# Gated mix of two attentions: exponents' tiles in one pool from the start, and additions of branch A moved to GpSimd

## The chip, the core and the metric

The kernel runs on one core of a Trainium2 chip. A core has TensorE (PE in the profile; its weight loads are the row PEld), VectorE (DVE), ScalarE (ACT), GpSimd (POOL) and SyncE (SP), which mostly issues DMAs; each works through a queue of its own in the order in which the program was written, and waits on semaphores for the others. SBUF is the working memory, PSUM (eight banks of 128 x 512 f32) takes what TensorE writes. The metric is the device time of one execution in microseconds, lower is better.

## The reference

x is 2048 x 512, and all is f32. Branch A is an attention in which each position looks at eight earlier ones, two apart; branch B has 32 heads of queries on one head of keys and values, over all 2048 positions. A gate from x mixes the two:

```python
def _A_ref(x, wqkv, wo):              # H = 32, Dh = 16, W = 8, dil = 2
    ...
    idx = pos[:, None] - off[None, :]
    ...
    logits = jnp.einsum("bhsd,bhswd->bhsw", q, kg) * scale
    logits = jnp.where(mask[None, None, :, :], logits, -1e9)
    attn = _softmax(logits, axis=-1)
    o = jnp.einsum("bhsw,bhswd->bhsd", attn, vg)
    ...
def _B_ref(x, wq, wk, wv, wo):        # one k and one v for all 32 heads
    ...
    scores = jnp.einsum("bhqd,bkd->bhqk", q, k) * (Dh ** -0.5)
    p = _softmax(scores, axis=-1)
    o = jnp.einsum("bhqk,bkd->bhqd", p, v)
    ...
g = _sigmoid((x * gate_w).sum(-1, keepdims=True))
return g * a + (1 - g) * b
```

## The kernel before

**Stages.** (1) Loads of x and weights; x and the weights are split into a high part and the rest (`xh`, `xl`, `wqh`, `wql`, `wah`, `wal`), so that three products in the fast f32r form replace one in f32. (2) The "front": `lumps` is a list of 14 projections of branch B's queries and 64 of branch A (`gg`, a group of eight heads, times `j`, one of 16 groups of positions). Each is 12 products whose two halves of 64 rows run beside each other into the two halves of one of the PSUM tiles `eb[0]`, `eb[1]` (`pe` in the profile). (3) 512 steps: in step s two pairs of score products go to `eb[0]` and `eb[1]` (`exp_pair`, L425), ScalarE takes their exponents into a tile `pexp` (L427), and the weighted sum of the step before (`weighted`, L435) adds four heads' products with `vst` in `po`. Sixteen steps make a unit: four heads of 512 queries, 32 units in all. (4) Four out phases (`out_phase`) between steps project finished rows and store them; a short tail does the last four row groups.

**Maxima.** The softmax of branch B needs each row's maximum first. These 2048 products (L301) are filled in wherever TensorE and the banks `m2` (`pm`) and `m1` (`ps`) are free, beside the front, the steps and the out phases; DVE reduces each straight from PSUM (L322 for a pair, L333 for a single one). In the front, once `half_keys` has formed half sums and half differences of keys (`kcd`), two blocks of keys are done in one: ScalarE takes the absolute value of a difference (L384, `dd`), and DVE adds the sum and reduces (L394). When a unit's maxima are complete, `filled` reduces and transposes them, and `shift_a`, `shift_c` and `shift_b` split them into two parts and write them with eight small DMAs (L414) into rows of the unit's query tile, where the score products subtract them. `stack(u)` loads a unit's query tile `qst` from DRAM (`qd`) with four DMAs on SP's queue; `queries_out` writes `qd` on the same queue.

**Branch A.** A projection's two halves are added by `a_post`: ScalarE copies one half from PSUM (L238), DVE adds the other (L243) into a `stage` tile of two positions, which an ACT-queue DMA stores to DRAM (`ad`). GpSimd then works through branch A's scores and values (`work`, a generator cut into pieces with costs in ns), for 32 pieces (g, hf); per piece DVE does the maximum over the eight positions (`a_max`) and the sum and reciprocal (`a_sum`, L530, L531), ScalarE the exponent.

**Order.** Nothing is scheduled at run time. A planner in the kernel's own Python keeps clocks for TensorE, ScalarE, DVE and GpSimd (`clk`, `pool`), times when banks come free (`free`) and tasks with due times (`tasks`, `hooks`), and writes each engine's instructions in the order that follows. `stream` interleaves the front or an out phase with maxima. `settle(kind, n)` runs tasks of a kind at once until n are left.

**Memory.** `xh` has four tiles of its own in pool `p1`, which is released when the front ends; the six `pexp` tiles of 128 x 1024 belong to a pool that is opened after that. The first step's exponents therefore go to a tile `early` that takes the place of `xh0`:

```python
if x == last and i == 4:
    early.append(p1.tile([P, 2, 2, 512], F32, name="early", tag="xh0", bufs=1))
    exp_pair(0, 0, early[0][:, 0])
```

Of the kernel before, what the change touches and what calls it, by code (L numbers as in the profile page):

```python
# [22 lines left out]
HG = 4  # L23
# [25 lines left out]
def gated_mix_kernel(ctx, tc, xt, wa, wk, wq, wo_a, wo_b, out):  # L49
# [64 lines left out]
    def split_x(t, eng):  # L114
        for c in range(C):
            split(xh[t][:, c, :], xl[:, t, c, :], xraw[t, c], eng)
# [64 lines left out]
    def queries(m):  # L181
        qb, cc = divmod(m, NHG // 2)
        cs = slice(cc * P, (cc + 1) * P)
        return three(lambda c: wqh[:, c, cs], lambda c: wql[:, c, cs], lambda c: xh[qb][:, c, :], lambda c: xl[:, qb, c, :])
# [9 lines left out]
    def queries_post(m, bank):  # L194
# [11 lines left out]
        def rest():  # L206
            nonlocal pool
            nc.scalar.activation(hi, own, AF.Copy)
            nc.gpsimd.tensor_sub(lo, own, hi.bitcast(F32))
# [10 lines left out]
    def a_project(gg, j):  # L220
        n = GN + (0 if gg else VN)
        t, r = j // 4, slice(j % 4 * P, (j % 4 + 1) * P)
        return three(lambda c: xh[t][:, c, r], lambda c: xl[:, t, c, r], lambda c: wah[gg][:, c, :n], lambda c: wal[gg][:, c, :n])

    def a_post(gg, j, x):

        bank, n = eb[x], GN + (0 if gg else VN)
        settle("post0", 0)
        settle("post1", 0)
# [4 lines left out]
        if gg == 0 and j < 3:  # L234
# [5 lines left out]
        free[f"e{x}"] = at + 1.5  # L240

        def rest():
# [4 lines left out]
            free[f"e{x}"] = after("dve", at, 0.5 if gg else 0.75) + 0.1  # L247
            if j % 2 == 1:
                dst = ad[gg * GC:(gg + 1) * GC, HALO:, :].rearrange("g (p j) n -> p g (j n)", j=NJ)
                tasks.append((free[f"e{x}"], lambda: nc.scalar.dma_start(dst[:, :, (j - 1) * AN:(j + 1) * AN], st.rearrange("p g j n -> p g (j n)")), (), "store"))  # L250
            if j == NJ - 1:
                tasks.append((free[f"e{x}"] + 0.5, whole, (gg,)))

        tasks.append((at, rest, (), f"post{x}"))

    def gates():
# [4 lines left out]
        for i in range(HG):  # L261
            for b in range(4):
                nc.scalar.activation(gate_t[32 * i:32 * i + 32, :, :, b], gate[32 * b:32 * b + 32, 1, :].rearrange("p (q j) -> p q j", j=4), AF.Copy)
# [74 lines left out]
    sel, kcd, dd, pend, ready_d, formed = [], [], [], [], [0.0, 0.0], set()  # L338
# [15 lines left out]
    def half_keys(g):  # L354
# [6 lines left out]
        clk["pe"] += 1.2  # L361
        for x in range(2):
            parts, src = kcd[0][:, g, x], hb[g][x]
            nc.scalar.activation(parts, src, AF.Identity, scale=mk[:, 0:1])
            at = after("act", clk["pe"] + T_LAT, 0.6)
            nc.vector.scalar_tensor_tensor(parts, src, mk[:, 1:2], parts.bitcast(F32), op0=ALU.mult, op1=ALU.add)
# [38 lines left out]
    def shift_c(v, mt, th, ml):  # L405
        nc.vector.scalar_tensor_tensor(ml, mt, mk[:, 5:6], th.bitcast(F32), op0=ALU.mult, op1=ALU.add)
        after("dve", 0, 0.45)
# [10 lines left out]
    pe, pexp, exped, early = [], {}, {}, []  # L418

    def exp_pair(s, pr, e=None):  # L420
# [5 lines left out]
        e = e or pe[0].tile([P, 2, 512], F32, name="pexp", bufs=6)  # L426
# [101 lines left out]
    def a_sum(g):  # L528
        asum[g] = p2[0].tile([P, NH, AG], F32, name="asum", bufs=2)
        nc.vector.tensor_reduce(asum[g], alog[g].rearrange("p w j h -> p j h w"), AX.X, ALU.add)  # L530
        nc.vector.reciprocal(asum[g], asum[g])  # L531
        after("dve", 0, 0.6)
# [107 lines left out]
    def stream(seq, mm, done, pooled):  # L640

        at, told = [0, 0], 0
        while min(at) < len(seq):
# [20 lines left out]
            if paired():  # L664
# [9 lines left out]
    def out_phase(js, n):  # L674

        prepare(js[0], n)
        turn(js[0], 1)
        later.pop(js[0])()
# [119 lines left out]
    def work():  # L798

        def sub(g, hf):  # L800
# [3 lines left out]
            hooks.append((pool + 5000, a_sum, g, ("sum", g, hf)))  # L804
            yield 500

        def values(g, hf):
            yield lambda: ("sum", g, hf) in done and (g < 8 or p2b)
# [11 lines left out]
        extra = list(wos)  # L820
        yield from load(0)
        yield from load(1)
        for i in range(0, len(order), 2):
            yield from a_scores(*order[i])
            hooks.append((pool + 3500, a_max, order[i][0], ("max",) + order[i]))
            for k, x in enumerate(a_scores(*order[i + 1])):
                yield x
                if k == 8:
                    yield from sub(*order[i])
            hooks.append((pool + 3500, a_max, order[i + 1][0], ("max",) + order[i + 1]))  # L830
            for k, x in enumerate(values(*order[i])):
                yield x
                if k == 8:
                    yield from sub(*order[i + 1])
            yield from load(i + 2)
# [36 lines left out]
    def mm(b, at):  # L872
# [3 lines left out]
        if x not in items:  # L876
# [10 lines left out]
            elif x == last:  # L887
                formed.clear()
            items[x] = queries(lump[1]) if lump[0] == "q" else a_project(*lump[1:])
            clk["pe"] = max(clk["pe"], free[f"e{x % 2}"])  # L890
# [3 lines left out]
        nc.tensor.matmul(eb[x % 2][:, b, :n], l[h], r[h], start=(i == 0), stop=(i == 3 * C - 1))  # L894
        return T_R if n == 512 else 0.18

    def done_mm(at):
# [7 lines left out]
        if x == last and i == 4:  # L905
            early.append(p1.tile([P, 2, 2, 512], F32, name="early", tag="xh0", bufs=1))
            exp_pair(0, 0, early[0][:, 0])
# [7 lines left out]
        else:  # L915
            gg, j = lump[1:]
            a_post(gg, j, x % 2)
# [8 lines left out]

    stream([(x, i) for x in range(len(lumps)) for i in range(3 * C)], mm, done_mm, True)
    assert not pend
    clk["pe"] += 0.7
    settle("post0", 0)  # L930
# [112 lines left out]
```

## Time and profile before

| what | value |
|---|---|
| median of three runs | 1550.73 us (1546.35 to 1551.43) |
| the profiled execution | 1548.13 us, of which its span 1546.4 us |
| TensorE weight loads | 720.5 us busy |
| front | 30 to 289 us |
| first and last weighted sum of the steps | 293.2 and 1534.1 us |
| out phases begin near | 878, 1146, 1289 and 1446 us |
| branch A on GpSimd | 147 to about 1050 us |

The span runs from the first to the last instruction. A row of the windows gives start and end, length, and then for each engine its busy time in that stretch and, in brackets, how many instructions it began; then the mean clock that TensorE was granted (1 is full speed), the share of DMA time and GB/s. A row of the waits gives the engine and line that waited, what ended the wait, the total in us, how often, and the longest one. A row of the timeline gives start, duration, engine, line, operation and tiles; the brackets tell the idle time before it and what ended that. A matmul's end is modelled, so that products that overlap look longer than the distance between their starts.

### The profile page before, as it was taken

The numbers are of one execution on the slowest core, as the hardware profiler recorded it, in microseconds if no ns is written. First come the engines' busy times: TensorE is split into PE (matmuls) and PEld (weight loads), VectorE is DVE, ScalarE is ACT, GpSimd is POOL, SyncE is SP. The second block draws the span as 40 slices with busy tenths as digits, with TensorE's granted clock in tenths as the row PEclk, the third lists the DMA queues.
The fourth block names the chain that finished last, engine by engine and source line by source line (L and its number), as shares of the span: only waits on it lengthen the run. The fifth ranks groups of instructions, "written<-read, shape, count | busy, mean of one in ns | idle before, by whom it ended". The sixth has DMA issues, their size and how long they took to land.

```text
span 1546.4 us, 29008 instructions
## 1 busy us (share of the span) xinstructions
PE 1498.4 (97%) x11020; PEld 720.5 (47%) x11020; DVE 1290.7 (83%) x1937; ACT 1220.0 (79%) x1490; POOL 934.7 (60%) x1525
## 2 busy tenths in 40 slices
PE   7899999899999999999999999999999999999997
PEld 4788999533333333333333453333345335433532
DVE  6887888789888989989898898998889889887811
ACT  4447776589999989999899749989875985799686
POOL 7731898698898888888889888884022003100310
PEclk9999999899999999999999999999999999999999
DMA  6643243221121122112112112110000000000000
GB/s 213 186 115 120 88 149 92 70 75 47 40 74 57 39 75 74 47 40 74 40 39 72 57 41 72 40 40 11 12 18 23 11 2 15 15 1 1 1 1 28
DMA packets 44019, 85.63 MB, mean 55 GB/s; under 512 B 9616, under 2 KB 26072, under 8 KB 39784
## 3 DMA queue, kind: packets, MB, share of 16 engines
q0 software_dynamic: 6816, 37.97, 7.4%
q1 hardware_dynamic: 19160, 31.40, 6.8%
q10 hardware_dynamic: 17904, 14.42, 2.9%
q8 instruction: 86, 1.41, 0.4%
q14 instruction: 53, 0.43, 0.1%
HBM read 57.97 MB, written 25.25 MB: 54 GB/s over the span
## 4 chain that ended last, share of the span: by engine, by line
PE 87%; ACT 5%; DVE 5%; DMA 1%; POOL 1%; issue 1%; SPq 1%; DVEq 0%; ACTq 0%; POOLq 0%
PE po L435 30%; PE pe L425 21%; PE pm L301 9%; PE pe L894 9%; PE ps L301 8%; PE pe L689 5%; ACT pexp L427 4%; DVE mx L322 2%; PE pm L375 2%; PE ps L375 1%; PE pe L172 1%; PE po L375 1%; DVE mx L333 1%; DMA xraw<-xt 0%; DMA qd<-qlo 0%
## 5 line engine op out<-in xcount | busy, mean ns | idle before, releaser
L427 ACT ACTIVATE pexp<-pe 128x1024 f32<-128x1024 f32 x1022 | 988.8, 1022 | 106.7 <-PE pe L425 100.2
L322 DVE TENSOR_REDUCE mx<-pm 128x2 f32<-128x1024 f32 x565 | 688.2, 1218 | 131.3 <-PE pm L301 126.7
L435 PE MATMUL po<-pexp,vst 128*32 128x512 f32 x4088 | 545.3, 605 | 0.5 <-ACT pexp L427 0.4
L425 PE MATMUL pe<-qst,kst 64*128 64x512 f32 x2048 | 467.1, 453 | 16.4 <-ACT pexp L427 7.6
L425 PEld LDWEIGHTS pe<-qst,kst 64*128 64x128 f32 x2048 | 191.8, 184 | 523.8 <-ACT pexp L427 503.4
L333 DVE TENSOR_REDUCE mx<-ps 128x1 f32<-128x512 f32 x556 | 377.6, 679 | 7.3 <-PE ps L301 6.6
L301 PE MATMUL pm<-kst,qst 62*128 62x512 f32 x1140 | 241.1, 410 | 3.2 <-DVE mx L322 1.9
L301 PE MATMUL ps<-kst,qst 62*128 62x512 f32 x556 | 227.5, 409 | 0.7 <-DVE mx L333 0.7
L495 POOL TENSOR_TENSOR pr<-aext 128x256 f32<-128x256 f32 x256 | 182.1, 737 | 4.7 <-PE pe L894 4.5
L548 POOL TENSOR_TENSOR oa<-oa,av 128x256 f32<-128x256 f32 x224 | 163.9, 732 | 17.3
L435 PEld LDWEIGHTS po<-pexp,vst 128*32 128x32 f32 x4088 | 80.4, 108 | 175.6 <-issue 162.3
L461 POOL TENSOR_TENSOR rl<-rl,gate_t 128x16 f32<-128x16 f32 x31 | 6.8, 219 | 249.7 <-DVE rl L455 249.7
L545 POOL TENSOR_TENSOR av<-aext,lg 128x256 f32<-128x256 f32 x224 | 139.3, 622 | 13.5
L301 PEld LDWEIGHTS pm<-kst,qst 62*128 62x128 f32 x1140 | 111.4, 187 | 28.1 <-DVE mx L322 23.0
L894 PE MATMUL pe<-wah,xh 64*128 64x384 f32 (+1 forms) x512 | 117.7, 349 | 4.8 <-DVE gate L246 3.3
L894 PE MATMUL pe<-wah,xl 64*128 64x384 f32 (+1 forms) x512 | 118.2, 342 | 0.0
L894 PE MATMUL pe<-wal,xh 64*128 64x384 f32 (+1 forms) x512 | 118.0, 342 | 0.0
L384 ACT ACTIVATE dd<-pm 128x512 f32<-128x512 f32 x162 | 88.5, 596 | 35.7 <-PE pm L375 31.8
L301 PEld LDWEIGHTS ps<-kst,qst 62*128 62x128 f32 x556 | 104.1, 187 | 26.6 <-DVE mx L333 21.1
L501 POOL TENSOR_TENSOR tr<-pr 128x512 f32<-128x512 f32 x64 | 81.6, 1276 | 4.9
L501 POOL TENSOR_TENSOR tr<-tr 128x256 f32<-128x256 f32 (+1 forms) x128 | 72.3, 565 | 9.2
L894 PEld LDWEIGHTS pe<-wah,xh 64*128 64x128 f32 x512 | 72.6, 190 | 10.8 <-issue 5.6
(157 smaller groups left out, 1523.3 us busy)
## 6 DMA issues: line engine op xcount, KB each, us to landing
aext<-ad POOLq DMA_DIRECT2D x32, 1056.0 KB, 5.5
ad<-stage ACTq DMA_DIRECT2D x32, 384.0 KB
qst<-qd SPq DMA_DIRECT2D x64, 128.0 KB
xraw<-xt SPq DMA_DIRECT2D x16, 256.0 KB
qd<-qhi SPq DMA_DIRECT2D x16, 256.0 KB
qd<-qlo SPq DMA_DIRECT2D x16, 256.0 KB
qst<-qd SPq DMA_DIRECT2D x64, 64.0 KB
qst<-ml SPq DMA_DIRECT2D x220, 2.0 KB
```

What stands on the lines that cost most here:

```text
L301: nc.tensor.matmul(dst, qst[v % NB][b:b + 62, pr, t * P:(t + 1) * P], kst[b:b + 62, kc * 512:(kc + 1) * 512], start=True, stop=True)
L322: nc.vector.tensor_reduce(m[:, :, pr, t, kc], dst, AX.X, ALU.max)
L333: nc.vector.tensor_reduce(m[:, odd, pr, t, kc:kc + 1], dst, AX.X, ALU.max)
L384: nc.scalar.activation(dd[0][:, odd], m2[:, odd, :], AF.Abs)
L425: nc.tensor.matmul(bank[:, odd, :], kst[b:b + 64, kt * P:(kt + 1) * P], qst[u % NB][b:b + 64, pr, :], start=True, stop=True)
L427: nc.scalar.activation(e, bank, AF.Exp, scale=SCALE)
L435: nc.tensor.matmul(po[32 * i:32 * i + 32, :], vst[:, kt, :], pexp[s, i // 2][:, i % 2, :], start=(kt == 0), stop=(kt == NJ - 1))
L495: nc.gpsimd.tensor_mul(pr[:, k], q, e[:, o:o + NH, AC:2 * AC])
L501: nc.gpsimd.tensor_add(nx, cur[:, :, 0:n], cur[:, :, n:2 * n])
L545: nc.gpsimd.tensor_mul(av, e[:, o:o + NH, 2 * AC:].rearrange("p j (h d) -> p j h d", d=DH), lg[:, w].unsqueeze(3).to_broadcast([P, NH, AG, ...
L548: nc.gpsimd.tensor_add(ao, ao, av)
L894: nc.tensor.matmul(eb[x % 2][:, b, :n], l[h], r[h], start=(i == 0), stop=(i == 3 * C - 1))
```

## The change

- The pool `px` with six tiles of 128 x 1024 is opened first and stays. In the front six of the eight half tiles of `xh` lie in it; the exponents' tiles come from it later. `early` is gone.
- The last projection of the front writes to `m2` in place of an `eb` tile, maxima end with the projection before it (`ended`), and both of step 0's pairs of scores are issued within it.
- For groups 1 to 3 of branch A, `a_add` replaces the DVE addition: ScalarE copies both halves to SBUF, GpSimd adds them, and the store goes out on SP's queue.
- The sum over the eight weights (`a_sum`) becomes three additions on GpSimd (`a_add_up`), with the reciprocal left on DVE; the low part of a shift (`shift_c`) becomes a product and a sum on GpSimd. A unit's two reductions in `filled` become one, which reads its input twice.
- The gate's sixteen small copies become tasks 3 us apart. The copies of `half_keys` become a task. `stack` for units 4 to 7 comes after projections 5, 7, 9 and 11 in place of two units after each of 2 and 3.
- An out phase is announced a step ahead: `prepare` runs then, and `turn` and its second half move into the first projection's products. The step after a phase keeps the usual order of its exponents.

```diff
+    px = ctx.enter_context(tc.tile_pool(name="exps", bufs=6))
...
-    xh = [p1.tile([P, C, 512], F32R, name="xh", tag=f"xh{t}", bufs=1) for t in range(NQB)]
+    xh = [[px.tile([P, 2, 512], F32R, name="xh", tag="pexp", bufs=6) for k in range(2)] for t in range(3)]
+    xh.append([p1.tile([P, 2, 512], F32R, name=f"xh3{k}") for k in range(2)])
...
             queries_out(m, hi, lo)
-            for u in (2 * m, 2 * m + 1):
-                if u < NB:
-                    stack(u)
+            if m > 4 and m % 2 and len(stacked) < NB:
+                stack(len(stacked))
...
+    def a_add(gg, j, x, st, bank, key):
+
+        settle("add", 1)
+        tag = ("two", "raw", "own")[j % 3]
+        two = (p2 if j % 3 else pm)[0].tile([P, GN], F32, name="two", tag=tag, bufs=1)
+        own = st[:, :, j % 2, :]
+        nc.scalar.activation(own, bank[:, 0, :GN].rearrange("p (g n) -> p g n", g=GC), AF.Copy)
+        nc.scalar.activation(two, bank[:, 1, :GN], AF.Copy)
+        at = after("act", clk["pe"] + T_LAT, 0.8)
+        free[key] = at + 0.1
+
+        def rest():
+            nonlocal pool
+            nc.gpsimd.tensor_add(own, own, two.rearrange("p (g n) -> p g n", g=GC))
+            pool = max(pool, 1e3 * at) + 1000
+            if j % 2 == 1:
...
+                tasks.append((pool / 1e3 + 0.5, lambda: nc.sync.dma_start(...), (), "store"))
...
-        for i in range(HG):
-            for b in range(4):
-                nc.scalar.activation(gate_t[32 * i:32 * i + 32, :, :, b], gate[32 * b:32 * b + 32, 1, :].rearrange("p (q j) -> p q j", j=4), AF.Copy)
+        for k in range(16):
+            tasks.append((clk["pe"] + 3.0 * (k + 1), gates_of, (32 * (k // 4), k % 4)))
...
-            for x in range(2):
-                nc.vector.tensor_reduce(ms[:, :, x, :], m, AX.X, ALU.max)
+            nc.vector.tensor_reduce(ms, m.unsqueeze(2).to_broadcast([P, 2, 2, 8, 4]), AX.X, ALU.max)
...
+        for k in keys:
+            free[k] = clk["pe"] + 4.0
+        tasks.append((clk["pe"] + 1.0, half_parts, (g, keys)))
...
-        nc.vector.scalar_tensor_tensor(ml, mt, mk[:, 5:6], th.bitcast(F32), op0=ALU.mult, op1=ALU.add)
+        nc.gpsimd.tensor_mul(mt, mt, mk[:, 5:6].to_broadcast([P, 32]))
+        nc.gpsimd.tensor_add(ml, mt, th.bitcast(F32))
...
     def a_sum(g):
-        asum[g] = p2[0].tile([P, NH, AG], F32, name="asum", bufs=2)
-        nc.vector.tensor_reduce(asum[g], alog[g].rearrange("p w j h -> p j h w"), AX.X, ALU.add)
         nc.vector.reciprocal(asum[g], asum[g])
+    def a_add_up(g):
...
+        nc.gpsimd.tensor_add(half, lgv[:, 0:4], lgv[:, 4:8])
+        nc.gpsimd.tensor_add(half[:, 0:2], half[:, 0:2], half[:, 2:4])
+        nc.gpsimd.tensor_add(asum[g].rearrange("p j h -> p (j h)"), half[:, 0], half[:, 1])
...
-        prepare(js[0], n)
-        turn(js[0], 1)
-        later.pop(js[0])()
...
+            if x == 0 and i == 1:
+                turn(j, 1)
+            if x == 0 and i == 6:
+                later.pop(j)()
...
-        if x == last and i == 4:
-            early.append(p1.tile([P, 2, 2, 512], F32, name="early", tag="xh0", bufs=1))
-            exp_pair(0, 0, early[0][:, 0])
+        if x == last - 1 and i == 3 * C - 2:
+            ended.add(1)
+        if x == last and i in (2, 7):
+            settle(f"post{(i - 1) % 2}", 0)
+            exp_pair(0, int(i == 2))
...
+    front = [(eb[0], "e0"), (eb[1], "e1"), (m2, "m2")]
```

More of the change, by code (lines that the diff above doesn't have):

```diff
@@ L233, in a_post @@
         st = stage["t"]
-        if gg == 0 and j < 3:
+        if gg:
+            return a_add(gg, j, x, st, bank, key)
+        if j < 3:
             two = wp.tile([P, GN + VN], F32, name="two", tag="aext", bufs=2)
@@ L642, in stream @@
         at, told = [0, 0], 0
+        ended.clear()
         while min(at) < len(seq):
@@ L893, in mm @@
         h = slice(64 * b, 64 * b + 64)
-        nc.tensor.matmul(eb[x % 2][:, b, :n], l[h], r[h], start=(i == 0), stop=(i == 3 * C - 1))
+        nc.tensor.matmul(front[2 if x == last else x % 2][0][:, b, :n], l[h], r[h], start=(i == 0), stop=(i == 3 * C - 1))
         return T_R if n == 512 else 0.18
@@ L916, in done_mm @@
             gg, j = lump[1:]
-            a_post(gg, j, x % 2)
+            a_post(gg, j, 2 if x == last else x % 2)
             if gg + 1 < C:
```

114 lines of the change are left out of this document (71 added, 43 removed).

## The prediction

> **What bounds the kernel now.** I read the page's engine totals first, then a table of windows, then TensorE's waits, then the timeline of the ordinary step and of the places where TensorE stood.
>
> ```profile
> PE 1498.4 (97%) x11020; PEld 720.5 (47%) x11020; DVE 1290.7 (83%) x1937; ACT 1220.0 (79%) x1490; POOL 934.7 (60%) x1525
> ```
>
> TensorE is the bound on average. Whether a stage has slack is told by the windows (length, then busy time and count of PE, PEld, DVE, ACT and POOL, then the granted clock):
>
> ```profile
> 40.00:67.00 27.00, 22.93 (x186) 19.00 (x184) 22.06 (x30) 9.80 (x15) 16.87 (x16) 0.94 0.65 186
> 147.00:158.00 11.00, 8.56 (x64) 8.00 (x64) 5.07 (x15) 7.03 (x19) 6.21 (x10) 0.69 0.69 250
> 158.00:283.00 125.00, 123.83 (x1282) 117.79 (x1278) 108.13 (x316) 90.15 (x185) 108.96 (x192) 1.00 0.38 116
> 283.00:300.00 17.00, 11.18 (x55) 6.17 (x57) 10.91 (x15) 6.38 (x7) 12.27 (x33) 0.68 0.11 35
> 300.00:306.00 6.00, 6.00 (x38) 2.15 (x30) 2.90 (x7) 3.63 (x7) 0.00 (x0) 0.78 0.00 0
> 400.00:500.00 100.00, 100.00 (x696) 35.83 (x690) 88.04 (x119) 92.30 (x103) 86.23 (x164) 1.00 0.14 48
> ```
>
> Between 158 and 283 us (branch A's projections) and in the steps (400 to 500) TensorE has no idle time: taking work off DVE there buys nothing by itself. But three windows have a clock below 1, and each begins with a wait of TensorE. Half clock for x us shows as a mean of 1 - x/2L: 3.2, 6.8, 10.9 and 2.6 us at half clock, of which half is lost: 12 us. The waits that TensorE's matmuls ended, in total:
>
> ```profile
> PE pe L425 <- ACT two L624: 5.0, 4, 1.5
> ...
> PE pe L894 <- ACT two L199: 4.1, 1, 4.1
> PE pe L894 <- DVE gate L246: 3.3, 3, 1.7
> PE pe L425 <- DVE stage L243: 2.6, 2, 1.7
> PE pm L375 <- ACT dd L384: 2.4, 1, 2.4
> ```
>
> The 4.1 us at 60 us goes back, through ScalarE, to GpSimd, and from there to a slow write of queries; the 2.4 us at 148 us to the gate's sixteen copies on ScalarE:
>
> ```profile
> 59.83 1.25 POOL L209 TENSOR_TENSOR qlo<-qraw,qhi 128x512 fp32r<-128x512 f32 x1 [6.12 <-DMA qd<-qlo]
> 145.20 3.82 ACT L263 ACTIVATE gate_t<-gate 32x16 f32<-32x16 f32 x16 [0.74 <-DVE gate L260]
> ```
>
> In the ordinary step the weighted sums start 2.13 us apart (414.32, then 416.46), TensorE has a matmul open throughout, and ScalarE's two exponents take 1.94 to 2.04 of it; the steps without maxima at the end (1488 to 1534 us) follow each other in 2.01.
>
> ```profile
> 414.32 1.07 PE L435 MATMUL po<-pexp,vst 128*32 128x512 f32 x8
> 415.92 1.94 ACT L427 ACTIVATE pexp<-pe 128x1024 f32<-128x1024 f32 x2
> 416.46 1.06 PE L435 MATMUL po<-pexp,vst 128*32 128x512 f32 x8
> ```
>
> **The change, part by part** (against the profiled execution, 1548.1 us: span 1546.4 and 1.7 around it; the median shown is 2.6 more, which I add at the end).
>
> *Loads of the queries.* Before, each of the projections q2 and q3 is followed on SP's queue by two units' reloads, eight issues of some 0.58 us that also wait for the write just ahead (the write of q4's high part goes out at 55.6 us; its data, L208 at 45.0, are ready at 45.6). The writes thus run ten us late and hold GpSimd's two buffers. The change puts one reload, of a unit written long before, behind every second projection from q5 on: per 7 us then 4 writes and 4 reads, 8 x 0.58 = 4.7 us of issue. The 4.1 us go, and with them half of 3.2 us: -5.7. If the writes themselves (2.95 to 3.4 us in the chain) are the limit, 0. I take -5.7, since the queue is served in order and the writes behind the reloads are the late ones.
>
> *The gate's copies* (L263, 228 ns each) go out one at a time some 3 us apart: ScalarE's work is the same, the block of 3.82 us is gone. Projections 2 and 3 of group 1 started 7.0 and 4.8 us before their followers, the mean one 2.87: 6.1 us in excess. -5.8, and -3 if another wait takes half.
>
> *Forming of the half keys* (around 110 us) moves behind the matmuls as a task: of the 3.3 us of L246 waits it can take the 1.75 at 110.8. -1.5 (0 to -3).
>
> *The passage to the steps.* From the start of the last projection (280.3) to the second step's weighted sum (299.3) 19.0 us pass, in which matmuls wait for ScalarE and DVE one after the other and 13.5 us have half the clock. After: the last projection (12 pairs, 2.1 us) writes to the maxima's banks, so that both banks of exponents are filled beside it; then ScalarE sets the pace with four exponents and two copies, 4 x 1.02 + 2 x 0.49 = 5.1 us from 0.6 us after its start, so the second weighted sum is at 6 to 8 us. I take 7.5: -11.5 (-13 to -3, the last if TensorE's wait for the two copies brings the half clock back).
>
> *Branch A's outputs, groups 1 to 3.* 48 DVE additions (L243, 552 ns: 26 us) leave DVE, which is no limit there; the 1.0 us that projections waited for them goes. ScalarE gets 48 more copies of 494 ns (L238), 23.7 us. Its queue serves the banks' release and the maxima's differences (two of 545 ns each): between 137 and 283 us it goes from about 105 to 126 of 140 us, nine tenths. Behind a copy that waits stand the differences, and behind these TensorE. From below -1 (all hidden), from above +23 (nothing hidden). As windows with 92% of ScalarE busy (400 to 500) leave TensorE without idle time, I take +3. GpSimd gets 48 additions of 128x384 (L76's of that shape 942 ns: 45 us) between branch A's pieces, and the 24 stores of them move from ScalarE's to SP's queue, behind the shifts' eight writes (5.31 us of issue at 874.7 us).
>
> *Sums of branch A's weights and the shifts' low parts.* DVE loses 32 x 359 ns (L530), 32 x 371 ns (L406) and, per unit, two short reductions of 215 ns (L312) for a single one that reads as much as L530 does, 359: 26 us in all. GpSimd gets 32 x (292 + some 240 + 217) and 32 x some 2 x 230 ns: 39 us. In the steps DVE's loss only counts where it made a step longer: over all steps the excess over 2.13 us is 21.7 us, and in steps that hold L530 or L406, or L312 with nothing else, 3.5 of it. -3.5 (0 to -7).
>
> L406 has a median of 249 ns and a longest of 1110. [...]
>
> *Out phases.* The first projection's parts are formed one step earlier and its transposes move behind its first matmuls. Of TensorE's waits the 1.2 us for GpSimd (L689 behind L584, once), the 1.7 us at L591 (4 times 0.4) go; of the 5.0 us behind the phases (L624) about half, because the next exponent takes the free bank first, though ScalarE must still do its copy of 1.03 us: -5 (-8 to 0).
>
> *Fills.* In the built order 21 of the 2048 maxima's matmuls move from the projections (442 to 421 there) to the steps: -21 x 0.115 on the one side, some 14 more full steps of 2.13 instead of 2.01 and one pause with three matmuls on the other: 0.
>
> GpSimd as a whole gets 84 us. Branch A now ends near 1050 us; at nine tenths busy 84 / 0.9 = 93 us later, near 1145. The cover is the third out phase, the first that needs all of it; in the built order it comes 15 steps earlier than before (1288 us), near 1225. Were it due earlier, each us that branch A is late would be a us of TensorE.
>
> Sum: -5.7 - 5.8 - 1.5 - 11.5 + 3 - 1 - 3.5 - 5 = -31.0; 1548.1 - 31.0 + 2.6 = 1519.7. Forecast 1520.
>
> [...]
>
> **Rivals.**
> ScalarE becomes the bound of the projections: for it the nine tenths and a fixed order of its queue, against it the 92% in the steps. +23 instead of +3: 1540. Chance 0.15.
> Waits come back at the passage and at the queries' writes (the same data must still move; against it, the causes named are gone): -3 for -11.5 and 0 for -5.7: 1534. Chance 0.12.
> Slower: branch A's tiles of outputs, two of them, refilled every two projections, come free too late. A tile has three projections, 8.6 us, from its last matmul to its next copy: copies 1.2, addition 0.95, issue 0.6 and a write like L189's of 3.4 leave 2.5 us, into which GpSimd's pieces ahead (0.62 to 1.29 each) and, five or six times, 5.3 us of the shifts' issues on SP must go. While the copy waits ScalarE stands, and after it TensorE. It decides from 1.3 us per tile on (24 x 1.3 = 31). With two pieces ahead of the addition and the store in line behind others a tile is some 3.5 us late, of which a us is hidden: 24 x 2.5 = 60, 1580. Against it: GpSimd is 87% busy in that window now, with waits that its planner accounts for. Chance 0.10.
>
> **How the numbers follow.** Forecast 0.62, the rivals 0.15, 0.12 and 0.10. 0.3% (4.7 us) is about what a measurement here can tell from no change. Faster than 1546: all of the first three but a few in 100 at their upper ends, 0.83; no change 0.06; slower, the jam and a little of the ScalarE case, 0.11. The range goes from all terms at their good ends (-44: 1507, and 2 for the spread of the runs) to ScalarE at its worst with half of the passage lost and the same 2 (1548).
>
> **What would show it.** Right: full clock at 60, 150 and 283 to 303 us; 7 to 8 us from the last projection to the second weighted sum; L591, L584 and L624 gone from TensorE's waits; projections 16 to 63 still 2.9 us apart. Wrong: projections over 3.1 us apart with TensorE waiting for the copies of L265 or L266, or ScalarE waiting for a DMA of the stage tile; a half clock at the passage; steps further apart than 2.13 us; an out phase that waits for GpSimd.

## The result, and the profile after

The changed kernel takes 1537.85 us (median of four runs, 1537.33 to 1539.43) beside 1548.54 for the kernel before on the same chip: a ratio of 0.9929 with a 95% interval of 0.9908 to 0.995. It is faster by 10.7 us, about a third of the 30.7 forecast. The time is inside the range; the sum behind the forecast is not borne out as it stood. The profiled execution has a span of 1537.6 us (before: 1546.4).

The engine totals of the changed kernel's page:

```profile
PE 1491.8 (97%) x11020; PEld 717.7 (47%) x11020; DVE 1250.2 (81%) x1794; ACT 1232.9 (80%) x1532; POOL 1016.9 (66%) x1725
```

DVE lost 40 us, GpSimd got 82: the work moved as planned. The windows of the prediction again, now of the changed kernel:

```profile
40.00:67.00 27.00, 27.00 (x235) 25.35 (x234) 27.00 (x36) 13.61 (x19) 23.23 (x21) 1.00 0.73 203
147.00:158.00 11.00, 10.94 (x115) 9.99 (x113) 6.53 (x23) 10.32 (x26) 10.72 (x16) 1.00 0.38 113
158.00:283.00 125.00, 109.33 (x1072) 105.11 (x1071) 68.89 (x213) 88.64 (x196) 95.27 (x149) 0.90 0.26 81
283.00:300.00 17.00, 13.86 (x119) 8.79 (x115) 8.26 (x21) 13.18 (x22) 12.78 (x25) 1.00 0.28 89
300.00:306.00 6.00, 6.00 (x49) 2.27 (x45) 5.09 (x7) 5.62 (x7) 5.69 (x16) 1.00 0.00 0
400.00:500.00 100.00, 100.00 (x702) 35.92 (x698) 89.11 (x111) 91.89 (x101) 84.97 (x168) 1.00 0.12 41
```

The three windows that had a low clock now have 1.00: the waits at 60, 148 and 283 us are gone. But the window between 158 and 283 us, which had hardly any idle time before, has lost 14.5 us of TensorE's busy time and a tenth of its clock. In it every engine does less; none has become the bound. So something stands that is not an engine's work. The waits that ended for TensorE's matmuls, and then those of ScalarE between 130 and 290 us:

```profile
PE pm L409 <- ACT dd L418: 15.0, 3, 6.4
...
PE pe L460 <- ACT pexp L462: 4.8, 17, 0.9
PE pe L460 <- ACT two L666: 2.9, 4, 1.0
```

```profile
ACT dd L418 <- PE pm L409: 19.8, 28, 1.6
ACT stage L265 <- DMA ad<-stage: 18.5, 4, 7.0
```

TensorE waited three times for a difference of ScalarE (L418), and ScalarE's copy of branch A's outputs (L265) waited four times for a store: it writes into a tile that the store has not yet read. ScalarE waiting for a DMA of this tile is a sign of being wrong that the prediction had named. The largest of TensorE's three waits, on the timeline from 190 us:

```profile
190.77 1.01 POOL L272 TENSOR_TENSOR stage<-stage,two 128x384 f32<-128x384 f32 x1
...
195.10 0.24 POOL L440 TENSOR_TENSOR mt<-mt,mk 128x32 f32<-128x32 f32 x1 [1.07 <-ACT mh L434]
195.42 0.25 POOL L441 TENSOR_TENSOR ml<-mt,mh 128x32 fp32r<-128x32 f32 x1
...
195.70 5.22 SPq L449 DMA_DIRECT2D qst<-ml  x8
...
200.97 0.95 SPq L276 DMA_DIRECT2D ad<-stage  x2
203.77 0.49 ACT L265 ACTIVATE stage<-pe 128x384 f32<-128x384 f32 x1 [7.01 <-DMA ad<-stage]
204.53 1.09 ACT L418 ACTIVATE dd<-pm 128x512 f32<-128x512 f32 x2
...
205.67 0.79 PE L409 MATMUL pm<-kcd,qst 62*128 62x512 f32 x2 [6.41 <-ACT dd L418]
```

Read it backwards. TensorE's product at 205.67 needs the bank that L418 reads; L418 stands behind L265 in ScalarE's queue; L265 needs the store, issued at 200.97. The tile of that store had been complete since the addition that ended at 191.78. In the 9.2 us between, SP's queue held the shift's eight writes ahead of the store: they waited for their data until 195.67 (L441), and then took 5.22 us to issue. Two stores, one for each of the only two tiles, stood behind them. The same picture is at 163.5 us (addition done 159.10, store 163.49) and 243.3 us (237.48, store 243.30).

By stage, from the starts of the projections and of the weighted sums (us; the last column is an experiment, `store_first`, told below):

| stage | before | after | store_first |
|---|---|---|---|
| to branch A's group 1 | 137.7 | 128.7 | 128.8 |
| groups 1 to 3, to the last projection's start | 142.6 | 158.7 | 134.2 |
| passage, to the second weighted sum | 19.0 | 9.9 | 10.0 |
| to the last weighted sum | 1234.9 | 1228.1 | 1230.6 |
| tail | 12.2 | 12.2 | 12.2 |
| span | 1546.4 | 1537.6 | 1515.7 |

All stages but one gained, 24.9 us together; groups 1 to 3 gave 16.1 back. They should have become 6 us shorter by the gate's copies, and so lost 22.

### The profile page after: what moved, and what is told of

It is laid out like the page before. It is cut to its first block, busy times and chain, and to the rows that moved or that the text cites. A ratio compares the mean times of both kernels' runs of the same rounds, so it can differ in the third digit from the quotient of the medians.

```text
span 1537.6 us, 29033 instructions
## 1 busy us (share of the span) xinstructions
PE 1491.8 (97%) x11020; PEld 717.7 (47%) x11020; DVE 1250.2 (81%) x1794; ACT 1232.9 (80%) x1532; POOL 1016.9 (66%) x1725
## 4 chain that ended last, share of the span: by engine, by line
PE 85%; DVE 5%; ACT 4%; POOL 2%; SPq 1%; DMA 1%; issue 1%; DVEq 0%; ACTq 0%; POOLq 0%
PE po L470 32%; PE pe L460 22%; PE pm L330 9%; PE ps L330 8%; PE pe L956 5%; PE pe L731 5%; ACT pexp L462 3%; DVE mx L350 3%; DVE mx L361 2%; SPq L449 1%; PE pe L174 1%; PE pm L409 1%; POOL stage L272 1%; DMA ad<-stage 1%; ACT dd L418 1%
## 5 line engine op out<-in xcount | busy, mean ns | idle before, releaser
L361 DVE TENSOR_REDUCE mx<-ps 128x1 f32<-128x512 f32 x568 | 385.8, 679 | 5.5 <-PE ps L330 4.7
L330 PE MATMUL ps<-kst,qst 62*128 62x512 f32 x568 | 230.6, 406 | 0.8 <-DVE mx L361 0.8
L587 POOL TENSOR_TENSOR av<-aext,lg 128x256 f32<-128x256 f32 x224 | 139.6, 623 | 13.5
L956 PE MATMUL pe<-wah,xh 64*128 64x384 f32 (+1 forms) x504 | 112.0, 349 | 3.0 <-DVE gate L249 1.7
L956 PE MATMUL pe<-wah,xl 64*128 64x384 f32 (+1 forms) x504 | 112.7, 347 | 0.0
L428 DVE CUSTOM_DVE_ANT_0 dd<-ps,dd 128x512 f32<-128x512 f32 x78 | 53.9, 691 | 71.6 <-PE ps L409 36.9
L956 PE MATMUL pe<-wal,xh 64*128 64x384 f32 (+1 forms) x504 | 111.9, 345 | 0.0
L418 ACT ACTIVATE dd<-pm 128x512 f32<-128x512 f32 x156 | 85.3, 600 | 28.6 <-PE pm L409 26.5
```

What stands on the lines that cost most here:

```text
L330: nc.tensor.matmul(dst, qst[v % NB][b:b + 62, pr, t * P:(t + 1) * P], kst[b:b + 62, kc * 512:(kc + 1) * 512], start=True, stop=True)
L361: nc.vector.tensor_reduce(m[:, odd, pr, t, kc:kc + 1], dst, AX.X, ALU.max)
L418: nc.scalar.activation(dd[0][:, odd], m2[:, odd, :], AF.Abs)
L587: nc.gpsimd.tensor_mul(av, e[:, o:o + NH, 2 * AC:].rearrange("p j (h d) -> p j h d", d=DH), lg[:, w].unsqueeze(3).to_broadcast([P, NH, AG, ...
L956: nc.tensor.matmul(front[2 if x == last else x % 2][0][:, b, :n], l[h], r[h], start=(i == 0), stop=(i == 3 * C - 1))
```

## The experiments

Each ran with the kernel before on the same chip. Kernels that ran on different chips are compared by their ratios to it, with the interval; the differences in us are of the medians.

**Which edit gained what, alone.** `b_stack` is the kernel before with the changed reloads, `b_gates` the kernel before with the gate's copies as tasks.

```diff
-            for u in (2 * m, 2 * m + 1):
-                if u < NB:
-                    stack(u)
+            if m > 4 and m % 2 and len(stacked) < NB:
+                stack(len(stacked))
```

> The kernel before with one edit: reloads of queries one unit behind every second projection from the sixth on. By the prediction the wait of 4.1 us at 60 us and the half clock after it go: -5.7, 1543 to 1545 beside 1549 to 1550 for before. If the queries' writes are the limit: no change.

1542.88 us, ratio 0.9954 [0.9938, 0.9971]: 6.4 us less. The projection that took 9.29 us takes 3.49. The forecast had -5.7.

```diff
-        for i in range(HG):
-            for b in range(4):
-                nc.scalar.activation(gate_t[...], ...)
+        for k in range(16):
+            tasks.append((clk["pe"] + 3.0 * (k + 1), gates_of, (32 * (k // 4), k % 4)))
```

> The kernel before with one edit: the gate's sixteen copies one at a time. By the prediction the wait of 2.4 us at 148 us and 6.8 us at half clock go: -5.8, 1543 to 1545. If another wait takes their place: -3 or less.

1546.73 us, 0.9988 [0.9978, 0.9998]: 2.6 us less where -5.8 was forecast. The two long projections are gone, but a(1,8), the projection of group 1 with j = 8, now takes 6.95 us: TensorE stands 2.7 us there for DVE's maximum (L397), and DVE had been held by one small instruction, the low part of a shift:

```profile
160.18 4.20 DVE L409 SCALAR_TENSOR_TENSOR ml<-mt,mk,mh 128x32 fp32r<-128x32 f32 x1
```

Its median in this kernel is 0.25 us. GpSimd's instructions followed each other without a gap from 160.02 to 164.33, and it ended at 164.38, when that row of them did. Alone, another wait took half, as the forecast's bound of -3 had it; in the full change, where the low part is GpSimd's, the two projections shrank by 5.4 us.

**Is it SP's queue?** `act_store` puts the stores of the changed kernel back on ScalarE's queue, `pool_store` puts them on GpSimd's.

```diff
-                ... lambda: nc.sync.dma_start(dst[...], st...)
+                ... lambda: nc.scalar.dma_start(dst[...], st...)     # pool_store: nc.gpsimd
```

> The changed kernel with the 24 stores of branch A's outputs (groups 1 to 3) issued from ScalarE's queue instead of SP's; TensorE's order is the same instruction for instruction. Theory (SP's queue): the three stalls of TensorE at 165, 199 and 242 us come from stores standing behind eight shift writes (5.2 us) on SP; they vanish, with the half clock behind them, and the time falls by 20 to 24 us to about 1515. Rival (GpSimd is late: the additions themselves come too late): the store waits as before, now on ScalarE, and the time stays at 1537 or rises. Rival (the transfers are slow): the tile comes free as late as before, 1537.

1531.19 us, 0.9889 [0.9868, 0.991]: 6.7 us less than the changed kernel, where the theory had 20 to 24. The first weighted sum comes at 280.6 us in place of 294.2. The three stalls are gone or under 2 us; others have come. On ScalarE's queue the last store's issue (281.82 us) waited for GpSimd's addition, and the exponent behind it (282.24) stood 1.6 us: at the passage TensorE stands 2.6 us with 6.8 us of half clock. And one store meets a load:

```profile
250.45 0.59 POOL L519 DMA_DIRECT2D aext<-ad  x1
250.79 0.37 ACTq L276 DMA_DIRECT2D ad<-stage  x1
```

Of the waits of the copy for a store, 9.2 us in all, the longest, 4.9 us, ends at 258.3, 7.5 us after this store's issue; its 384 KB were under way beside the 1056 KB of L519, issued 0.3 us before. Elsewhere issue and landing lie 2.8 us apart (200.97 to 203.77 above). That the load beside it is the cause was not tried by itself.

> The same with the 24 stores issued from GpSimd's queue, right behind the additions in order. SP's queue: stalls vanish, about 1515; GpSimd's 24 issues of 0.58 us (14 us) are hidden. GpSimd is late: 24 more issues make the additions later still, above 1537.

1550.46 us, 1.0012 [1.0002, 1.0022]: no gain left at all, the first weighted sum at 303.5 us. ScalarE's copies still wait for stores, 23.8 us in 11 places (longest 4.7) where the changed kernel had 18.5 in four: an issue takes 0.8 us on GpSimd (0.36 on SP), the issues and the additions are in one queue, and behind late copies TensorE has gaps of up to 3.1 us and 20 us of half clock. This is the time that the rival (GpSimd is late) had named; so `pool_store` does not tell SP's queue from that rival.

**Shorter writes.** `shift_split` leaves the stores on SP and gives four of the eight shift writes to GpSimd while branch A runs, as both kernels do after it.

```diff
-                (nc.gpsimd if b and not pieces else nc.sync).dma_start(...)
+                (nc.gpsimd if b else nc.sync).dma_start(...)
```

> The changed kernel with half of each unit's eight shift writes on GpSimd's queue also while branch A runs, so that SP holds a store for 2.6 us instead of 5.2. SP's queue: the three waits of ScalarE for the stage tile (3.2, 7.0 and 6.3 us) each shrink by about 2.6 us or to nothing, about half of the loss comes back: 1523 to 1530. Other causes: no change from 1537.

1548.04 us, 0.9992 [0.9981, 1.0004]. The front gained: the first weighted sum is at 282.6 us, and the three stalls of 2.8, 6.4 and 5.8 us shrank by 1.5, 2.6 and 2.8, as the theory of SP's queue had it. But the steps lost 21 us (1249.3 us between the second weighted sum and the last, against 1228.1). One of the places:

```profile
547.39 2.30 POOL L449 DMA_DIRECT2D qst<-ml  x4 [0.35 <-POOL ml L441]
...
550.44 0.22 POOL L574 TENSOR_TENSOR asum<-half 128x16 f32<-128x16 f32 x1
...
550.69 0.25 DVE L564 RECIPROCAL asum<-asum 128x16 f32<-128x16 f32 x1 [3.28 <-POOL asum L574]
```

This shows a price of another part of the change. Since the weights' sums are GpSimd's, DVE's reciprocal waits for them, and the maxima behind it too: 2.3 us of issues on GpSimd cost DVE 3.3 us and TensorE 2.5.

**The additions on DVE again.** `dve_add` takes `a_add` back (DVE adds, the stores on ScalarE, one copy on ScalarE in place of two); all else stays changed.

```diff
-        if gg:
-            return a_add(gg, j, x, st, bank, key)
-        if j < 3:
+        if gg == 0 and j < 3:
```

> The changed kernel with the addition of branch A's outputs back on DVE and its stores on ScalarE's queue, as before the change; all else stays changed. If the move of the additions is what took the rest of the gain, and DVE was no limit there: 1513 to 1520, as with the store moved. If relief of DVE is worth something in the projections: 5 us or more slower than the kernel with the store on ScalarE.

1526.06 us, 0.9852 [0.9832, 0.9871]: 11.8 us less than the changed kernel. So `a_add`, with its stores where they were, cost this much net. One projection of 8 us is left, a(1,10), and it is not a store's landing that ScalarE waits for:

```profile
159.04 0.25 POOL L439 TENSOR_TENSOR ml<-mt,mh 128x32 fp32r<-128x32 f32 x1
159.32 5.37 SPq L447 DMA_DIRECT2D qst<-ml  x8
161.05 0.37 ACTq L251 DMA_DIRECT2D ad<-stage  x1
161.52 0.49 ACT L239 ACTIVATE two<-pe 128x384 f32<-128x384 f32 x1 [3.86 <-DMA qst<-ml]
```

ScalarE was idle for 3.86 us before L239, and nearly all of it lies before its own store's issue at 161.05 (L251). The kept trace has this store and the first of SP's eight writes count on the same completion semaphore (number 101); the write was issued at 159.32 and landed at 160.98, and the store went out at 161.05, although its tile had been complete since 157.08 and it reads nothing of the write. `dve_add_shift` also puts the shift's low part back on DVE, and `dve_all` the weights' sums as well.

> The kernel dve_add (additions of branch A's outputs back on DVE, stores on ScalarE's queue; 1526.1) with the shifts' low part back on DVE as well. Theory (a DMA waits for an earlier one): dve_add's one long projection (8.0 us in place of 2.8, at 159 us, half clock after it) is ScalarE's store waiting for the landing of a shift write that uses the same DMA semaphore, and that write waits for GpSimd's low part, late behind branch A's pieces. With the low part on DVE the wait goes: 1519 to 1523. Rival (the eight writes themselves are too slow): the long projection stays, 1526.

1532.27 us, 0.9883 [0.9869, 0.9898]. The projection of 8 us is gone (first weighted sum 2.8 us earlier than in `dve_add`), but the steps take 1240.6 us where `dve_add` has 1231.2. The planner wrote another order, with a pause (a step that is held for maxima) of 11.1 us at step 471 where `dve_add` has 5.7; and step 76 takes 5.6 us, with 3.4 us of half clock behind it. That one is no pause:

```profile
439.08 4.07 DVE L438 SCALAR_TENSOR_TENSOR ml<-mt,mk,mh 128x32 fp32r<-128x32 f32 x1
```

The low part, back on DVE, took 4.07 us beside a row of GpSimd instructions that ended at 443.10, as in `b_gates`, and TensorE stood 2.6 us for the maximum behind it. The median is 0.25 us here too; over all 32 the mean is 0.59, where the kernel before has 0.37. How much L440 and L441 on GpSimd gain in all can't be read from this run, because of the other order.

> The same with the sums of branch A's weights back on DVE too, so that no addition of the change is left on GpSimd and only the other edits remain. If the sums on GpSimd are worth what the prediction took for them, some 2 of its 3.5 us: 2 us slower than dve_add_shift. If DVE's load counts more than its longer steps showed: 5 us or more slower. If it does not count: the same.

1535.14 us, 0.9902 [0.9887, 0.9917]; span 1531.4 beside 1530.4, with the same two long steps (L438 took 3.95 us at the first). The intervals of the two overlap; by the spans 1 us, by the medians 2.9, are what the weights' sums on GpSimd gain. The forecast's part for them (about half of -3.5) is of this size, but not shown to be more than nothing.

**Queue, lateness, or who waits?** With DVE's additions the stores were on another queue and earlier, and the tile was first written by DVE. `dve_add_sp` only moves the stores of `dve_add` to SP. `own_copy` then makes ScalarE's copy the first writer of the tile, as in the changed kernel; `own_copy2` adds ScalarE's second copy, its result unused.

```diff
+        # dve_add_sp
-                ... nc.scalar.dma_start(dst[...], st...)
+                ... (nc.sync if gg else nc.scalar).dma_start(dst[...], st...)
+        # own_copy
+        if gg:
+            two = st[:, :, j % 2, :]
+        # own_copy2
+        if gg:
+            more = pm[0].tile([P, GN + VN], F32, name="two", bufs=1)
+            nc.scalar.activation(more[:, :n], bank[:, 1, :n], AF.Copy)
```

> The kernel with DVE's additions (1526.1 us, first weighted sum at 276.6 us) with one edit: the stores of groups 1 to 3 go out on SP's queue, as in the changed kernel. Theory 1, the place in SP's queue behind the shifts' eight writes (5.2 us of issue) is what made the copies wait, whoever adds: waits of ScalarE for the DMA of the stage tile of 3 to 7 us come back at two or three places, each with a half clock behind it; first weighted sum at 283 to 292 us, time 1532 to 1541. Theory 2, the lateness of GpSimd's additions was needed for it (a store handed over 2 to 3 us earlier stands before the eight writes more often and leaves slack when it does not): first weighted sum at 275 to 279, time 1524 to 1529.

1525.93 us, 0.9863 [0.9847, 0.9878], no difference to `dve_add` in time. But groups 1 to 3 take 146.2 us in place of 142.7, and the first weighted sum at 280.3 us is later than the second theory had it; the passage is 2.1 us shorter, since the last store no longer stands on ScalarE. DVE's wait for the tile and, in `own_copy`, ScalarE's, from 130 to 290 us:

```profile
DVE stage L244 <- DMA ad<-stage: 8.4, 3, 3.3
```

```profile
ACT stage L241 <- DMA ad<-stage: 11.9, 4, 4.0
```

So stores behind the eight writes delay the tile here too; but the longest wait is 3.3 us, not 7.0, and DVE has the time: it is busy 75% of 158 to 283 us.

> The kernel with DVE's additions and the stores on SP (1525.9 us), where ScalarE's copy goes straight into the tile of outputs, as in the changed kernel, and DVE adds the other half to it there: the same copies, additions and stores, and only another engine that writes to the tile first. In the kernel before in this row the tile's waits for a store were DVE's (8.4 us in three places) and cost TensorE little. Theory 1, it matters who waits: ScalarE's copy now stands in those places, the differences behind it in ScalarE's queue and then TensorE too: 8 to 15 us of waits of the copy for the DMA, half clock behind them, first weighted sum at 281 to 290 us, time 1530 to 1538. Theory 2, only the lateness of GpSimd's additions mattered: first weighted sum at 274 to 279, 1524 to 1528.

1528.92 us, 0.9877 [0.9855, 0.9898]. The waits are ScalarE's now and of the size that the first theory gave; the time lies between the two theories. The ratios' intervals overlap, so the times alone don't show a difference; in the traces groups 1 to 3 take 5.5 us more (146.2 and 151.7). Who waits matters there, and is the smaller part.

> The kernel with DVE's additions into ScalarE's copy (1528.9 us, first weighted sum near 287) with ScalarE's second copy of the changed kernel brought back, its result unused: 48 times 0.49 us, 23.5 us more on ScalarE, written where the second copy stands in the changed kernel. Theory 1, that ScalarE's added work is hidden (the prediction's +3): 0 to 4 us slower, 1528.5 to 1533. Theory 2, the rival of ScalarE as the bound of the projections: 8 to 23 us slower, 1537 to 1552, with matmuls waiting for ScalarE's differences in many small gaps.

1532.22 us, 0.99 [0.9882, 0.9918]; the front is not longer (second weighted sum at 287.1 us, 288.9 in `own_copy`), the profiled span the same 1528.2. ScalarE is busy 17.1 us more (a copy overlaps the one before it, so that 48 of them add 0.36 us each rather than 0.49). By the ratios the two kernels can't be told apart, and the stage is not longer (151.7 and 150.1 us): the copies are hidden in the projections, and ScalarE as their bound falls as a rival.

**The place in the queue alone.** `store_first` is the changed kernel, with GpSimd's additions, SP's queue and both copies, except that a pending addition and its store are put out before a shift's eight writes.

```diff
     def shift_b(v, ml):
+        settle("add", 0)
+        settle("store", 0)
         for b in range(2):
```

> The changed kernel (1537.9 us, first weighted sum at 294.2 us) with one edit: before a shift's eight writes are put into SP's queue, any pending addition of branch A's outputs and its store are put out. GpSimd's additions, SP's queue and both of ScalarE's copies stay as they are. Theory 1, the place in the queue is the cause, and GpSimd's additions matter because they make the store's turn come after the writes: two of the three stalls go (the waits of ScalarE's copy for the DMA fall from 18.5 to under 8 us), first weighted sum at 278 to 286 us, time 1523 to 1531. Theory 2, GpSimd's additions are late in themselves or ScalarE is too full: the stalls stay under another name, first weighted sum at 289 to 295, 1533 to 1539.

1516.34 us (1514.87 to 1517.47), 0.9791 [0.9777, 0.9806]: 21.5 us less than the changed kernel, and better than the first theory's range. ScalarE's copies wait for a store once, for 0.4 us. The same 195 us region, some five us earlier on this kernel's clock, where the two stores now precede the writes:

```profile
186.87 5.07 SPq L276 DMA_DIRECT2D ad<-stage  x2
...
190.10 0.25 POOL L441 TENSOR_TENSOR ml<-mt,mh 128x32 fp32r<-128x32 f32 x1
...
191.99 5.21 SPq L451 DMA_DIRECT2D qst<-ml  x8
```

Windows of the changed kernel, then of `store_first`:

```profile
200.00:241.00 41.00, 35.33 (x345) 34.12 (x346) 23.50 (x73) 29.75 (x65) 29.82 (x44) 0.88 0.25 75
241.00:262.00 21.00, 15.24 (x141) 14.53 (x140) 9.02 (x27) 11.50 (x25) 11.89 (x16) 0.84 0.35 117
```

```profile
200.00:241.00 41.00, 41.00 (x435) 39.52 (x434) 27.94 (x88) 35.61 (x78) 38.66 (x56) 1.00 0.37 115
241.00:262.00 21.00, 21.00 (x228) 20.75 (x227) 14.54 (x45) 18.39 (x40) 19.48 (x27) 1.00 0.40 130
```

In both kernels TensorE's and DVE's instructions have the same order; ScalarE has one store of group 0, and GpSimd one addition, one place earlier; on SP, at each of the four shifts in this stage, one store (at the second, two) stands ahead of the eight writes in place of behind them. Five stores of 24 make the difference: TensorE is now busy throughout at full clock, with ScalarE at 87% and GpSimd at 94% of the first of these windows. That settles the cause. The writes go out 1.6 us after their data are ready (191.99 against 190.35), and nothing waits for that.

`dve_first` makes the same edit in `dve_add_sp`.

> The kernel with DVE's additions and the stores on SP (1525.9 us) with the same edit as store_first: pending additions and stores are put out before a shift's eight writes. Theory 1, the place of the stores was its only loss too, and where the additions run matters little: 1515 to 1520, within 4 us of store_first (1516.3 us), first weighted sum at 268 to 273. Theory 2, the additions belong on GpSimd, DVE holds up the projections: 1521 to 1527, with TensorE waiting for DVE's additions. Theory 3, DVE's additions are the better place: under 1514.

1521.18 us, 0.9812 [0.9795, 0.9828]. The edit gained some 8 us here (0.9863 to 0.9812), where it gained 21.5 in the changed kernel, and long projections are left: two stores still stand behind the writes at 267 us, and on SP the edit moved a single store, the one before the shift at 228 us. Whether DVE or GpSimd is the better place for the additions can't be told from this: 0.9791 against 0.9812, with intervals that overlap.

**The passage and the pause.** `dve_add_last` puts the last projection's store alone on SP, so that the first exponents don't stand behind its issue on ScalarE; `best1` also moves the pause near step 471 one step later, with two maxima instead of three; `best2` does the latter in `store_first`.

```diff
-                ... nc.scalar.dma_start(...)
+                ... (nc.sync if gg == C - 1 and j == NJ - 1 else nc.scalar).dma_start(...)
+        # best1 and best2
-        steps = 16 * v - 6 - s
+        steps = 16 * v - 5 - s
```

> The kernel with DVE's additions and its stores on ScalarE (1526.1 us), where the last projection's store alone goes out on SP. Theory: at the passage ScalarE's last store issue waits for the addition, and the first step's exponents stand behind it (TensorE idle 1.6 us, then 3.4 us at half clock): without it the passage from the last projection's start to the second weighted sum gets 2 to 3 us shorter, 1523 to 1524.5. Rival: the exponents wait for something else there (the copies of the last projections, the banks): no change, 1525.5 to 1527.

1522.14 us, 0.9839 [0.9823, 0.9856]; `dve_add_sp`, beside it on the same chip, 1525.93. From the first to the second weighted sum 2.7 us pass in place of 4.7, and no half clock is left at the passage: as the theory had it. Against `dve_add` itself the ratios' intervals overlap; the spans are 1524.5 and 1520.8.

> The kernel before in this list with the pause near step 471 put one step later and made two maxima long in place of three. The pause cost 5.7 us in the kernel with DVE's additions, and 6.8 us of half clock are within or behind it. Theory, the clock is lost because the chain product, reduction, shift, exponent leaves TensorE idle whatever the pause holds: the pause still costs 4 to 6 us, no change against the kernel before in this list (within 1.5 us). Rival, the length of the idle time goes with the number of maxima: 2 to 3 us less, 1520 to 1522.

1519.03 us, 0.9819 [0.9805, 0.9834]. The step with the pause takes 4.0 us in place of 5.7, and the half clock behind it is gone. The windows of `dve_add` and of `best1`:

```profile
1380.00:1415.00 35.00, 32.92 (x208) 11.29 (x205) 27.33 (x34) 26.71 (x29) 3.60 (x8) 0.90 0.01 2
```

```profile
1380.00:1415.00 35.00, 33.61 (x238) 11.86 (x234) 29.04 (x34) 30.32 (x33) 3.44 (x8) 1.00 0.01 1
```

> store_first (1516.3 us) with the pause near step 471 put one step later and made two maxima long in place of three, as in the kernel that this took from 1522.1 to 1519.0 us. In store_first the pause costs 5.7 us, and 6.8 us of half clock begin there, the only ones left before the tail. Theory, the same gain again: 2 to 4 us, 1512 to 1514.5. Rival, the gain there was by chance of the order: 1515 to 1518.

1513.31 us (1513.09 to 1513.74), 0.9765 [0.9751, 0.978], 3.0 us less than `store_first` by the medians. The ratios' intervals just overlap; in the traces the steps take 1226.3 us in place of 1230.6 and no half clock is left before the tail: the same gain. It is the fastest kernel of the study, 36.8 us under the kernel before on that chip.

## Why the prediction was wrong, step by step

**Loads of the queries** (-5.7): right. -5.8 in the trace, -6.4 as an edit alone.

**The gate's copies** (-5.8): right in the full change, -5.4; alone only -2.6, because the low part of a shift then held DVE for 4.20 us at another place.

**Half keys** (-1.5): undersized; the two projections near 110 us went from 4.72 and 4.66 us to 3.52 and 2.20, -3.7.

**The passage** (7.5 us): 9.9 measured, so -9.1 instead of -11.5. The mechanism was right (no half clock, 13.5 us of it before), the 7.5 too short.

**Branch A's outputs, groups 1 to 3** (+3 and -1.0): this is the step that failed. The stage lost 22 us against it. The prediction asked whether ScalarE's 48 copies are hidden, and answered right: `own_copy2` and `store_first` show that they are. But +3 carried nothing for the last half sentence of that step, the 24 stores that move "from ScalarE's to SP's queue, behind the shifts' eight writes (5.31 us of issue at 874.7 us)". There the 5.3 us were seen, and not followed: on SP the store at 200.97 went out behind the eight writes put ahead of it, and these had waited until 195.67 for data of their own. The store lost 3.9 us to that wait and 5.3 to the issues. With one edit in this order alone, the stage takes 134.2 us and the whole change gives -30.7 us of span, where the sum said -31.0. That agreement is partly luck: the stage then does 4.6 us better than forecast (-8.4 against -3.8), which makes up for the passage and the steps.

**The slower rival** had the mechanism (two tiles, the store behind other issues, ScalarE and then TensorE stand) and the wrong price. It charged every one of 24 tiles with 2.5 us. In truth most tiles lost nothing, and those that met a shift's writes lost more: the four projections concerned lie 4.6, 8.2, 7.5 and 1.9 us over the mean of 2.8, those after them 3.1 together, 25 us in all. Of that 15.0 us is idle time at the first three and 2.1 at the fourth; the rest is the half clock behind it (6.8, 10.2 and 6.8 us, partly over the idle time). The rival's own words "five or six times, 5.3 us of the shifts' issues" came close to the count, which is four.

**Sums and shifts** (-3.5): undersized. The steps' excess over 2.13 us fell from 21.7 to 15.8 without the step of the pause, -5.9 (18.9 with it); by `dve_all` 1 to 3 us of this may be the sums, which the runs don't set apart from nothing. L406's longest in the kernel before, 1.11 us (1012.14 to 1013.25), lay beside a GpSimd instruction that ended at 1013.20; elsewhere the low part took far longer on DVE: 4.20 us in `b_gates`, 4.07 and 3.95 in the two kernels that move it back. There it stopped TensorE for 2.5 to 2.7 us each time; what held it was not tried by itself, and what it was worth over all steps was not separated.

**Out phases** (-5): right, -4.9 (143.8 to 139.0 us for the four).

**Fills** (0): wrong by the pause. Its step takes 5.2 us, 3.1 more than another; in some kernels a half clock of 6.8 us follows. One line makes 3 us of it good.

**GpSimd's 84 us hidden**: right, +82 busy, and no out phase waits for it. But the weights' sums tie DVE to GpSimd's queue, which `shift_split` brought to light.

## What to carry to other kernels

When a transfer changes its queue, ask what stands ahead of it in program order there, what those issues themselves wait for, and how many tiles are left while they do: count the meetings, not the mean. If every engine gets less busy in a stage that got longer, look for a queue whose head waits, and try the order of issues before moving the work back: two lines were worth 21.5 us here, moving the additions back 11.8. A planner that keeps clocks for engines and none for the queue of DMAs will not see this.

## What the runs showed of the hardware

The half clock came in stretches of 3.4, 6.8 and 10.2 us, but for the one that the end of the span cuts off: in the kernel before at 64 us (3.4), 149 (6.8), 286 (3.4) and 292 (10.2), in the changed kernel at 167 us (6.8), 201 (10.2) and 246 (6.8). The shortest single idle time of TensorE with one behind it was 1.44 us (at 983 us in `shift_split`); in the kernel before it was 1.70 us (at 285 us), and two of 0.89 and 1.12 us close together had one behind them, at 292 us. And it does not follow each: the pause's 1.77 us brought 6.8 us of half clock in `dve_add` and in `store_first` and none in the changed kernel, and 3.2 to 3.3 us at 160 us brought 3.4 us in `dve_add` and none in `best1`. So the length of one idle time did not tell in these runs whether the half clock came.

Eight writes of 2 KB took 5.2 us of SP's queue, 0.65 us each; a store of 384 KB behind them cost 0.36 to issue. The loss lay in the wait and the issues ahead of the stores, not in the bandwidth: in the window from 200 to 241 us the DMA engines were 25% busy with the stores late (the changed kernel) and 37% with them in time (`store_first`).

In `dve_add` a store on ScalarE's queue stood until a 2 KB write of SP's queue had landed (160.98, the store's issue 161.05), whose data it does not use; both count on semaphore 101. A kernel with other semaphores for them was not run.

A DVE instruction with a median of 0.25 us (the low part of a shift) took 3.95 to 4.20 us in three kernels. In `b_gates` and `dve_add_shift` it ended 0.05 us after GpSimd's row of instructions beside it (164.38 and 164.33 us, 443.15 and 443.10).
